# Scoring two heads at once, the queries' second parts in 64-row matmuls side by side

## The chip, the cores and the metric

The kernel runs on one core of a Trainium2 chip. The metric is the device time of one execution in microseconds (us); the time before is the median of three runs, 733.85 us (732.66 to 736.66). One further execution was recorded by the hardware profiler. TensorE is called PE, VectorE DVE, ScalarE ACT, GpSimd POOL and SyncE SP; PEld is TensorE's loading of weights, the stationary operand of a matmul.

## What is computed

Local attention with a few global keys and a bias that falls with the distance, over 4 sequences of 768 positions and 8 heads of 64 elements, and then a gated two-layer network on the result (3072 tokens, 512 wide, 1536 hidden):

```python
scores = scale * np.matmul(q, k.transpose(0, 1, 3, 2))
keep = is_global | is_local            # key j: j < 8, or 0 <= i - j < 96
scores = np.where(keep, scores - slopes[h] * dist, -1e9)
a = softmax(scores)
x = np.matmul(a, v)                    # heads side by side: 3072 x 512
out = ((x @ w_a) * (x @ w_b)) @ w_out
```

Everything is float32. A product of two float32 matrices is made from parts that TensorE multiplies in one pass: each operand is cut into a first part (rounded to the type float32r) and a second part (what is left), and the products of first with first, first with second and second with first are added up.

## The kernel before

**Units.** The 24 blocks of 128 queries are dealt into eight units: unit 0 has the first block of each sequence (4 blocks), unit 1 has 2 blocks, units 2 to 7 have 3 each. A query block needs a window of keys only: 232 keys (its own 128, the 96 before and the 8 global ones), or 128 for the first block of a sequence. For each unit the kernel computes attention, and then the network on the unit's tokens (`moe`, 12 steps of 128 hidden columns). While unit u is in the network, the attention of unit u + 1 is computed in between.

**The network** (L1042 and L1060) is TensorE's main load: per step two projections of 12 matmuls each, whose moving operand is as wide as the unit has tokens (512, 256 or 384), and per block three matmuls of 512 columns back into the accumulators acc.

**Attention of units 2 to 7** (`attention`, called late units below). Heads are taken one by one. For each head, SP loads a tile raw, whose rows 0 to 63 hold the head's queries (transposed) and one half of its keys, and whose rows 64 to 127 hold the same queries again and the other half of the keys. `split` (L582) makes three tiles of it: qh, the queries' first part, scaled, on all 128 rows; ql, their second part, also on all 128 rows; kk, in which each key column has its first part on one half of the rows and its second part on the other half. With this layout one matmul of 128 rows gives the queries' first part times both parts of the keys. For every window (a block and a head) there are two matmuls into the bank psS (L953): qh with kk, then ql with kk. DVE adds the bias to the scores and takes the row's extreme (L659, which reads the bank), ACT takes the exponential (L676), the row is divided by its sum (L708 or L710), DVE transposes blocks of 32x32 (L752), and 16 small transfers per pair of heads put those blocks in place in a tile pf (L766). Then the product with the values v (L787, `values`): a stationary operand of 64 columns, the even head of a pair in the columns 0 to 63 and the odd one in 64 to 127. Values of two pairs of heads are done in one go (JOINT = 2), into the banks psA and psT. L787 is float32 without parts; the trace lists two instructions for each float32 matmul.

**Attention of units 0 and 1** (`quad`) uses raw float32 tiles with two heads on the two halves of the rows: scores by matmuls of 64 rows (L821), the two heads into two banks, transposes on TensorE (L735), values by L787. This part is not touched by the change.

**The order of the work** is written by a planner inside the kernel. Every operation has a due time, a cost for each engine that may do it, and the buffers that it reads and writes; `Schedule.order` walks through modelled time and gives each engine its next operation whose inputs and buffers are there. The costs are constants in the code: `pe(n)` is n / 2.23 + 2.5 ns, and a score operation of a late unit has `2 * pe(w)`. A list of numbers, MOVES, shifts the due times of some operations of the first two units at random by fixed seeds. The result is a fixed order for each engine; on the chip an engine works through its list and waits where an input isn't there.

**Buffers that the change touches.** kk, qh and raw have two buffers, ql one, pf two. TensorE's eight result banks are psS, psT, psA, acc0 to acc2, p0 and p1, one buffer each.

## Time and profile before

| | |
|---|---|
| median of three runs | 733.85 us (732.66 to 736.66) |
| the profiled execution: its own time | 731.68 us |
| its span, first to last instruction | 729.8 us |
| granted TensorE clock | 0.999 |
| busy: PE / PEld / DVE / ACT / POOL | 97% / 88% / 66% / 48% / 1% |
| PE's work ends at | 723.5 us of the span |
| matmul instructions on PE | 4356 |

A row of the timeline gives the start and the duration of a group of instructions that follow each other. A matmul's duration includes its way through the array, during which the next ones already run, so what a matmul costs is read from the distance between two starts, not from its duration. "64*128" in a row is the shape of the stationary operand, rows by columns.

### The profile page before, as it was taken

What the parts mean: (1) busy time and instruction counts of PE and PEld (TensorE: products, weight loads), DVE (VectorE), ACT (ScalarE), POOL (GpSimd) and SP (SyncE); (2) the same over time, 40 slices, a digit from 0 to 9 for tenths busy, and PEclk for the clock granted to TensorE, in tenths of its full rate; (3) what the DMA queues carried; (4) which work ended last, traced back from release to release, by engine and by line L of the source; (5) the groups of instructions that cost most, each with busy time, mean ns of one, the idle gap of its engine ahead of it and who ended that gap; (6) DMA issues with size and microseconds to landing.
All of it is one profiled execution on the core that took longest, in us unless ns stands there. A gap on an engine that the chain in (4) does not pass through costs nothing.

```text
span 729.8 us, 12598 instructions
## 1 busy us (share of the span) xinstructions
PE 708.6 (97%) x4356; PEld 639.2 (88%) x4356; DVE 483.1 (66%) x1560; ACT 353.1 (48%) x907; POOL 5.9 (1%) x16
## 2 busy tenths in 40 slices
PE   5899999999999999999999999999999999999996
PEld 4577777899899999999899999998999999999996
DVE  6999999779975873587726967278662896321111
ACT  5999776364553552555426544263443554221111
POOL 3000000000000000000000000000000000000000
PEclk9999999999999999999999999999999999999999
DMA  7899100134543343134331343224432243110001
GB/s 269 316 380 364 41 17 28 42 101 127 170 137 81 90 129 108 64 89 125 89 104 65 106 129 108 65 85 106 135 101 86 65 128 88 45 44 1 1 1 48
DMA packets 38552, 78.06 MB, mean 107 GB/s; under 512 B 8528, under 2 KB 21072, under 8 KB 38480
## 3 DMA queue, kind: packets, MB, share of 16 engines
q1 hardware_dynamic: 28960, 67.33, 28.8%
q10 hardware_dynamic: 9520, 9.84, 5.3%
q8 instruction: 36, 0.59, 0.3%
q14 instruction: 36, 0.29, 0.1%
HBM read 51.97 MB, written 6.29 MB: 80 GB/s over the span
## 4 chain that ended last, share of the span: by engine, by line
PE 84%; DVE 5%; ACT 3%; DMA 3%; ACTq 2%; issue 1%; SPq 1%; DVEq 0%; POOL 0%; POOLq 0%
PE p L1042 49%; PE acc L1060 24%; PE pa L787 5%; PE ps L953 4%; DMA pf<-wm 3%; ACTq L766 2%; DVE t L659 1%; ACT t L676 1%; DVE wm L752 1%; ACT wr L516 1%; PE pt L735 1%; PE ps L821 1%; SPq L766 1%; DVE kk L447 1%; PE acc_2b L1060 1%
## 5 line engine op out<-in xcount | busy, mean ns | idle before, releaser
L1042 PE MATMUL p<-xh,wt 128*128 128x384 f32 (+2 forms) x1488 | 419.5, 337 | 1.4 <-ACT raw L437 0.9
L1042 PEld LDWEIGHTS p<-xh,wt 128*128 128x128 f32 x1488 | 271.0, 188 | 15.2 <-ACT raw L437 1.9
L1042 PE MATMUL p<-xl,wt 128*128 128x384 f32 (+2 forms) x816 | 269.7, 340 | 0.7 <-ACT xl L437 0.5
L1060 PE MATMUL acc<-wt,hh 128*128 128x512 f32 (+1 forms) x576 | 203.4, 390 | 0.0
L1042 PEld LDWEIGHTS p<-xl,wt 128*128 128x128 f32 x816 | 153.4, 188 | 10.8 <-ACT xl L437 0.8
L1060 PEld LDWEIGHTS acc<-wt,hh 128*128 128x128 f32 x576 | 108.3, 188 | 20.0 <-issue 1.6
L1081 DVE TENSOR_TENSOR raw<-p,raw 128x384 f32<-128x384 f32 (+2 forms) x96 | 52.9, 551 | 90.5 <-PE p L1042 89.7
L676 ACT ACTIVATE t<-t,sm 128x232 f32<-128x232 f32 (+1 forms) x120 | 55.3, 464 | 116.7 <-DMA pf<-wm 71.3
L1060 PE MATMUL acc<-wt,hl 128*128 128x512 f32 (+1 forms) x288 | 111.7, 388 | 0.0
L437 ACT COPY raw<-p 128x384 f32<-128x384 f32 (+2 forms) x71 | 34.4, 485 | 122.3 <-PE p L1042 116.2
L447 DVE TENSOR_TENSOR hl<-raw,hh 128x384 fp32r<-128x384 f32 (+2 forms) x96 | 52.8, 550 | 11.1 <-ACT hh L437 10.4
L1060 PEld LDWEIGHTS acc<-wt,hl 128*128 128x128 f32 x288 | 54.2, 188 | 6.6
L659 DVE CUSTOM_DVE_ANT_0 t<-ps,rel 128x232 f32<-128x232 f32 x74 | 28.8, 389 | 39.2 <-PE ps L953 38.4
L447 DVE TENSOR_TENSOR kk<-raw,kk 64x348 fp32r<-64x348 f32 x96 | 49.6, 516 | 3.6 <-ACT kk L437 0.5
L437 ACT CAST hh<-raw 128x384 fp32r<-128x384 f32 (+2 forms) x72 | 37.3, 519 | 19.8 <-DVE raw L1081 19.6
L787 PE MATMUL pa<-pf,v 128*64 128x128 f32 x640 | 41.5, 278 | 1.7 <-ACT pf L437 1.4
L787 PEld LDWEIGHTS pa<-pf,v 128*64 128x64 f32 x640 | 35.9, 138 | 7.2 <-issue 3.5
L953 PE MATMUL ps<-kk,qh 128*128 128x232 f32 x144 | 39.8, 277 | 1.5 <-DVE sm L659 1.5
L708 ACT ACTIVATE wm<-wm,sm 128x232 f32<-128x232 f32 x58 | 27.9, 487 | 24.6 <-DVE sm L698 23.9
L953 PE MATMUL ps<-kk,ql 128*128 128x232 f32 x144 | 39.5, 274 | 0.0
L676 ACT ACTIVATE wm<-wm,sm 128x232 f32<-128x232 f32 x72 | 34.7, 483 | 5.7 <-DVE sm L659 5.1
L708 ACT ACTIVATE t<-t,sm 128x232 f32<-128x232 f32 (+1 forms) x76 | 34.6, 477 | 5.1 <-DVE sm L698 4.0
(84 smaller groups left out, 687.4 us busy)
## 6 DMA issues: line engine op xcount, KB each, us to landing
wr<-wts SPq DMA_DIRECT2D x24, 768.0 KB, 10.9
raw<-qkv SPq DMA_DIRECT2D x48, 366.0 KB, 3.0
v<-qkv SPq DMA_DIRECT2D x24, 384.0 KB, 3.2
pf<-wm ACTq DMA_DIRECT2D x192, 48.0 KB, 2.0
pf<-wm SPq DMA_DIRECT2D x192, 48.0 KB, 1.9
out<-o SPq DMA_DIRECT2D x23, 256.0 KB, 2.0
v<-qkv SPq DMA_DIRECT2D x8, 256.0 KB, 3.9
raw<-qkv SPq DMA_DIRECT2D x3, 512.0 KB, 8.0
```

Of the source, the lines that this page charges most:

```text
L437: self.nc.scalar.copy(out(), src())
L447: lambda e: self.engine(e).tensor_sub(out(), a(), b()),
L516: lambda e, low=low: nc.scalar.activation(low(), low().bitcast(U32), AF.Copy, scale=2.0**-29),
L659: lambda e, j=j, o=o, w=w, neg=neg, at=at: nc.vector.tensor_tensor_reduce(t[:, o : o + w], ps[:, o : o + w], neg[:, at : at + w], -scale, ...
L676: lambda e, j=j, o=o, w=w: nc.scalar.activation(t[:, o : o + w], t[:, o : o + w], AF.Exp, bias=sm[:, j : j + 1], scale=-1.0, accum_out=sm[ ...
L708: nc.scalar.mul(t[:, o : o + w], t[:, o : o + w], r)
L766: lambda e, out=out, src=src: self.queue(e).dma_start(out(), src()),
L787: nc.tensor.matmul(pa[D * s : D * s + D, i * P : i * P + P], v[:, v0 : v0 + D], probs[s, i][1](c), start=c == 0, stop=c == len(slots) - 1,)
L953: nc.tensor.matmul(ps[:, :w], q[:, i * P : i * P + P], kk[:, k0 : k0 + w], start=m == 0, stop=m == 1,)
L1042: nc.tensor.matmul(p[:, :T], wt(), b[:, b0 : b0 + T], start=c == 0 and n == 0, stop=c == NCC - 1 and n == 2,)
L1060: nc.tensor.matmul(acc[:, :n], hs[:, i * P : i * P + P], wt(), start=f == 0 and k == 0, stop=f == NF - 1 and k == 2,)
L1081: lambda e, asb=asb, pb=pb: nc.vector.tensor_mul(asb[:, :T], pb[:, :T], asb[:, :T]),
```

## The change

**Scores.** The heads of a late unit are taken by pairs. The two raw tiles of a pair are packed differently: one has the first half of both heads' keys, the other the second half, the even head on rows 0 to 63 and the odd head on rows 64 to 127 (the queries of a tile are still those of one head, twice). `split` makes qh and kk for both heads, and one ql for the pair: the even head's second part on the rows 0 to 63, the odd head's on 64 to 127. In a head's kk, the keys' first part now stands on the rows of the head's own half for all columns. A score operation serves one block and both heads: qh with kk for the even head into psS, the same for the odd head into psT, then ql with kk on 64 rows for each of the two heads, into the same two banks. The product of the queries' second part with the keys' second part is left out. The planner's cost is `3 * pe(w) + 10`.

**Values** are done for one pair of heads at a time, always into psA. The results of the pairs 2 and 3 go into the pair's own pf tile instead of new tiles.

MOVES is another list. Softmax, transposes, transfers, the network and the units 0 and 1 have the same operations as before; the numbers of matmuls are the same.

```diff
@@ -40,10 +40,7 @@
 CHUNKS = 12
 SQ = 32
 
-JOINT = 2
-
-SHORT = PAIRED
-OLD = ()
+PBUFS = 2
 
 
 HOMES = "kk sm raw hh v wm hl xh xl o qh pf ql t"
@@ -76,7 +73,7 @@
...
-MOVES = (1010, 1025, 1037, 1048, 1089, 1106, 1156, 1251, 1276, 1371, 1475, 1603, 1662, 1754, 1881, 11792, 12402, 7, 26, 46, 60, 85, 142, 169, 213, 252, 392, 531, 549, 595, 835, 995, 2161, 2240, 11001)
+MOVES = (8, 33, 56, 90, 167, 201, 230, 264, 328, 358, 418, 533, 564, 621, 754, 4891, 5013, 5338, 5407)
...
@@ -579,51 +576,57 @@
         )
         return v
 
-    def split(self, u, h, due, raw):
+    def split(self, u, c, due, raws):
+
 
 
         nc, pl, op = self.nc, PLANS[u], self.plan.op
         nq, hk = pl.nb * P, pl.nk // 2
-        n = f"{u}_{h}"
-        reads = [raw]
-        sc = 2.0 ** (h - 2)
-        qh = self.sbuf([P, MAXQ], F32R, "qh", "qh" + n, 2)
-        ql = self.sbuf([P, MAXQ], F32R, "ql", "ql" + n)
-        kk = self.sbuf([P, MAXK], F32R, "kk", "kk" + n, 2)
-
-        def scale(e):
-            if e == "act":
-                nc.scalar.mul(qh[:, :nq], raw[:, :nq], sc)
-            else:
-                nc.vector.tensor_scalar_mul(qh[:, :nq], raw[:, :nq], sc)
-
-        op(due, scale, reads, [qh], port=BOTH, act=act(nq), dve=dve(nq, True))
-        op(
-            due,
-            lambda e: nc.vector.scalar_tensor_tensor(
-                ql[:, :nq], raw[:, :nq], sc, qh[:, :nq], op0=ALU.mult, op1=ALU.subtract
-            ),
-            reads + [qh],
-            [ql],
-            port=BOTH,
-            dve=dve(nq),
-        )
-        for half in range(2):
-            a, o = slice(64 * half, 64 * half + 64), slice(64 - 64 * half, 128 - 64 * half)
+        halves = slice(0, 64), slice(64, 128)
+        ql = self.sbuf([P, MAXQ], F32R, "ql", f"ql{u}_{c}")
+        qhs, kks = [], []
+        for s, raw in enumerate(raws):
+            h = 2 * c + s
+            sc = 2.0 ** (h - 2)
+            qh = self.sbuf([P, MAXQ], F32R, "qh", f"qh{u}_{h}", 2)
+            qhs.append(qh)
+            kks.append(self.sbuf([P, MAXK], F32R, "kk", f"kk{u}_{h}", 2))
+
+            def scale(e, raw=raw, qh=qh, sc=sc):
+                if e == "act":
+                    nc.scalar.mul(qh[:, :nq], raw[:, :nq], sc)
+                else:
+                    nc.vector.tensor_scalar_mul(qh[:, :nq], raw[:, :nq], sc)
+
+            op(due, scale, [(raw, "q")], [qh], port=BOTH, act=act(nq), dve=dve(nq, True))
+            op(
+                due,
+                lambda e, raw=raw, qh=qh, sc=sc, a=halves[s]: nc.vector.scalar_tensor_tensor(
+                    ql[a, :nq], raw[a, :nq], sc, qh[a, :nq], op0=ALU.mult, op1=ALU.subtract
+                ),
+                [(raw, "q"), qh],
+                [(ql, s)],
+                port=BOTH,
+                dve=dve(nq),
+            )
+
+        for half, raw in enumerate(raws):
             cols = slice(half * hk, half * hk + hk)
-            src = lambda a=a: raw[a, pl.k0 : pl.k0 + hk]
-            hi = lambda a=a, cols=cols: kk[a, cols]
-            self.copy(due, hi, src, hk, reads, [(kk, (half, 0))])
-            self.sub(
-                due,
-                lambda o=o, cols=cols: kk[o, cols],
-                src,
-                hi,
-                hk,
-                reads + [(kk, (half, 0))],
-                [(kk, (half, 1))],
-            )
-        return qh, ql, kk
+            for s, kk in enumerate(kks):
+                a, o = halves[s], halves[1 - s]
+                src = lambda raw=raw, a=a: raw[a, pl.k0 : pl.k0 + hk]
+                hi = lambda kk=kk, a=a, cols=cols: kk[a, cols]
+                self.copy(due, hi, src, hk, [(raw, "k")], [(kk, (half, 0))])
+                self.sub(
+                    due,
+                    lambda kk=kk, o=o, cols=cols: kk[o, cols],
+                    src,
+                    hi,
+                    hk,
+                    [(raw, "k"), (kk, (half, 0))],
+                    [(kk, (half, 1))],
+                )
+        return qhs, ql, kks
 
     def dist(self, h):
 
@@ -906,7 +909,7 @@
             self.result(1, c, due + step, pa, x)
 
     def probs32(self, name):
-        return self.sbuf([P, CHUNKS * P], F32, "pf", name, JOINT)
+        return self.sbuf([P, CHUNKS * P], F32, "pf", name, PBUFS)
 
     def result(self, u, c, due, pa, x):
         nq, (xc, x0) = PLANS[u].nb * P, x[c]
@@ -929,72 +932,65 @@
             x += [(self.probs32(f"x{u}_{c}"), 0) for c in range(2, NCC)]
             self.second(x, start, end)
             return x
-        step = (end - start) / H
+        step = (end - start) / NCC
+        each = sum(len(slots) for slots in pl.vslot)
         groups = []
         for c in range(NCC):
+            due = start + c * step
             probs = {}
-            v = self.fetch_v(u, c, start + (2 * c + 1) * step - LOADLEAD)
+            v = self.fetch_v(u, c, due + step / 2 - LOADLEAD)
             pf = self.probs32(f"pf{u}_{c}")
+            raws = [self.fetch(u, 2 * c + s, due - LOADLEAD) for s in range(2)]
+            qhs, ql, kks = self.split(u, c, due - SPLITLEAD, raws)
             slot = 0
-            old = u == SHORT and c in OLD
-            for s in range(2):
-                h = 2 * c + s
-                due = start + h * step
-                raw = self.fetch(u, h, due - LOADLEAD)
-                qh, ql, kk = self.split(u, h, due - SPLITLEAD, raw)
-                for i in range(pl.nb):
-                    due = start + h * step + (i + 1) * step / pl.nb
-                    k0, w = pl.kwin[i]
-                    n = f"{u}_{h}_{i}"
-                    ps = self.bank("psS", "ps" + n)
-
-                    def scores(e, i=i, k0=k0, w=w, ps=ps, qh=qh, ql=ql, kk=kk):
-                        for m, q in enumerate((qh, ql)):
-                            nc.tensor.matmul(
-                                ps[:, :w],
-                                q[:, i * P : i * P + P],
-                                kk[:, k0 : k0 + w],
-                                start=m == 0,
-                                stop=m == 1,
-                            )
-
-                    op(due, scores, [qh, ql, kk], [ps], pe=2 * pe(w), spare=SPARE)
-                    turn = (pl.nb * h + i) % (TBUFS + len(self.spares))
+            for i in range(pl.nb):
+                due = start + c * step + (i + 1) * step / pl.nb
+                k0, w = pl.kwin[i]
+                n = f"{u}_{c}_{i}"
+                ps = [self.bank(tag, f"{tag}{n}") for tag in ("psS", "psT")]
+
+                def scores(e, i=i, k0=k0, w=w, ps=ps, qhs=qhs, ql=ql, kks=kks):
+                    qs = slice(i * P, i * P + P)
+                    for s in range(2):
+                        nc.tensor.matmul(
+                            ps[s][:, :w], qhs[s][:, qs], kks[s][:, k0 : k0 + w], start=True, stop=False
+                        )
+
+                    for s in range(2):
+                        r = slice(64 * s, 64 * s + 64)
+                        nc.tensor.matmul(
+                            ps[s][:, :w], ql[r, qs], kks[s][r, k0 : k0 + w], start=False, stop=True
+                        )
+
+                op(due, scores, [*qhs, ql, *kks], ps, pe=3 * pe(w) + 10, spare=SPARE)
+                chunks = len(pl.vslot[i])
+                for s in range(2):
+                    h = 2 * c + s
+                    turn = (2 * (pl.nb * c + i) + s) % (TBUFS + len(self.spares))
                     if turn < TBUFS:
-                        t = self.sbuf([P, 2 * P], F32, "t", "t" + n, TBUFS)
+                        t = self.sbuf([P, 2 * P], F32, "t", f"t{s}{n}", TBUFS)
                     else:
                         t = self.spares[turn - TBUFS]
-                    sm = self.sbuf([P, 8], F32, "sm", "sm" + n, 6)
+                    sm = self.sbuf([P, 8], F32, "sm", f"sm{s}{n}", 6)
                     dist = lambda w: (self.negd if w > P else self.negd0, 0)
                     done = [(self.wm, k) for k in range(MBUFS)]
-                    self.softmax(due, [(0, w)], ps, t, sm, dist, 2.0 ** -(h + 1), done, REST)
-                    chunks = len(pl.vslot[i])
-                    if old:
-                        pt = self.bank("psT", "pt" + n)
-                        self.turn(due, [(0, w)], t, pt, pf, slot * P, SPARE)
-                    else:
-                        self.blocks32(due, w, t, slot, chunks)
-
-                    def get(k, slot=slot, pf=pf, old=old):
-                        if old:
-                            return pf[:, (slot + k) * P : (slot + k + 1) * P]
+                    self.softmax(due, [(0, w)], ps[s], t, sm, dist, 2.0 ** -(h + 1), done, REST)
+                    at = s * each + slot
+                    self.blocks32(due, w, t, at, chunks)
+
+                    def get(k, at=at, pf=pf):
                         view = pf[:, :].rearrange("p (a m i) -> p m a i", a=P // SQ, m=CHUNKS)
-                        return view[:, slot + k]
+                        return view[:, at + k]
 
                     probs[s, i] = (pf, get)
-                    slot += chunks
-            due = start + (2 * c + 2) * step
-            if not old:
-                self.swap(due, pf, slot)
-            pa = self.bank(("psA", "psT")[c % JOINT], f"pa{u}_{c}")
-            groups.append((v, probs, pa))
-            if len(groups) == JOINT:
-                self.values(due, pl, range(pl.nb), groups)
-                if len(x) <= c:
-                    x += [(self.probs32(f"x{u}_{k}"), 0) for k in range(2, NCC)]
-                for k, (_, _, pa) in enumerate(groups, c + 1 - JOINT):
-                    self.result(u, k, due, pa, x)
-                groups = []
+                slot += chunks
+            due = start + (c + 1) * step
+            self.swap(due, pf, 2 * each)
+            pa = self.bank("psA", f"pa{u}_{c}")
+            self.values(due, pl, range(pl.nb), [(v, probs, pa)])
+            if len(x) <= c:
+                x.append((pf, 0))
+            self.result(u, c, due, pa, x)
         return x
 
     def moe(self, u, start, step, x):
@@ -1443,8 +1439,9 @@
         if u >= PAIRED:
             hk = pl.nk // 2
             for h in range(H):
-                rows = (kt[h][:, :hk], kt[h][:, hk:])
-                put(QOFFS[u][h], np.vstack([np.hstack([qt[h], half]) for half in rows]))
+                half = slice(h % 2 * hk, h % 2 * hk + hk)
+                pair = kt[h - h % 2], kt[h - h % 2 + 1]
+                put(QOFFS[u][h], np.vstack([np.hstack([qt[h], k[:, half]]) for k in pair]))
         else:
             for c in range(NCC):
                 cols = []
```

**How the order on PE changes.** The first place is in unit 3's attention, in between the network of unit 2 (xh and p are the network's, acc its accumulators). Before, the two matmuls of one window, for head 2 and block 1, with the network's ahead and behind:

```order
L1060 MATMUL acc2_2_2786<-wt1_1_764,hl2_1_2796 128x512
L1060 MATMUL acc2_2_2786<-wt1_1_764,hh2_1_2790 128x512
L953 MATMUL ps3_2_1_2871<-kk3_2_2635,qh3_2_2627 128x232
L953 MATMUL ps3_2_1_2871<-kk3_2_2635,ql3_2_2808 128x232
L1042 MATMUL p02_3_2874<-xh2_2606,wt3_0_941 128x384
L1042 MATMUL p02_3_2874<-xl2_2613,wt3_0_941 128x384
```

Now the operation for block 1 and the heads 2 and 3:

```order
L1038 MATMUL p12_3_2864<-xh2_2598,wt3_1_978 128x384
L955 MATMUL psS3_1_1_2906<-kk3_2_2793,qh3_2_2785 128x232
L955 MATMUL psT3_1_1_2908<-kk3_3_2795,qh3_3_2787 128x232
L961 MATMUL psS3_1_1_2906<-kk3_2_2793,ql3_1_2798 128x232
L961 MATMUL psT3_1_1_2908<-kk3_3_2795,ql3_1_2798 128x232
L1056 MATMUL acc2_0_2750<-wt2_1_848,hh2_2_2844 128x512
```

Two of the four score matmuls (L961) now have a stationary operand of 64 rows; ahead of them and behind them stand matmuls of 128 rows. There are 144 score operations before and 72 now, all of this form.

The second place is the end of unit 2's attention, where the values of its pairs 2 and 3 are. Before:

```order
L1042 MATMUL p02_0_2622<-xh2_2606,wt0_0_636 128x384
L787 MATMUL pa2_2_2651<-pf2_2_2325,v2_2_2312 64x128 x12
L787 MATMUL pa2_3_2664<-pf2_3_2536,v2_3_2341 64x128 x12
L1060 MATMUL acc1_0_1791<-wt11_1_1572,hh1_11_2620 128x512
L1060 MATMUL acc1_0_1791<-wt11_1_1572,hl1_11_2637 128x512
```

Now, pair 2 some 65 rows earlier, and pair 3:

```order
L1038 MATMUL p01_10_2466<-xl1_1701,wt10_0_1531 128x256
L1038 MATMUL p01_10_2466<-xh1_1682,wt10_0_1531 128x256
L790 MATMUL pa2_2_2488<-pf2_2_2363,v2_2_2044 64x128 x12
L1038 MATMUL p01_10_2466<-xh1_1682,wt10_0_1531 128x256
...
L1056 MATMUL acc1_1_1844<-wt11_1_1627,hh1_11_2609 128x512
L790 MATMUL pa2_3_2650<-pf2_3_2545,v2_3_2274 64x128 x12
L1038 MATMUL p02_0_2621<-xh2_2598,wt0_0_636 128x384
```

What was one block of 24 matmuls of 64 columns is now two blocks of 12, each between the network's matmuls; over the late units there are 24 such blocks instead of 12.

## The prediction

> **What bounds the kernel now.** I read the page's totals first, then busy time by stage, then the waits of TensorE (PE), then single starts on PE. From the page:
>
> ```profile
> span 729.8 us, 12598 instructions
> PE 708.6 (97%) x4356; PEld 639.2 (88%) x4356; DVE 483.1 (66%) x1560; ACT 353.1 (48%) x907; POOL 5.9 (1%) x16
> PE 84%; DVE 5%; ACT 3%; DMA 3%; ACTq 2%; issue 1%; SPq 1%; DVEq 0%; POOL 0%; POOLq 0%
> ```
>
> The busy times of stretches of the span (the stretch, its length, then the engines); the late units' attention lies in the second of them:
>
> ```profile
> 42.00:145.00 103.00, 103.00 (x512) 81.49 (x511) 98.46 (x191) 74.84 (x136) 0.00 (x0) 1.00 0.37 139
> 145.00:640.00 495.00, 492.85 (x3181) 458.56 (x3180) 331.68 (x1174) 226.67 (x628) 0.00 (x0) 1.00 0.36 100
> 640.00:723.50 83.50, 83.44 (x472) 79.10 (x470) 16.58 (x31) 17.20 (x35) 0.00 (x0) 1.00 0.03 10
> ```
>
> From 145 to 640 us PE stands still for 2.2 us of 495, and DVE, the next one, is busy for 67%. So whatever the change adds to PE or takes from it there comes out at the end one for one, unless another engine becomes late. PE's longest waits, by sum (us, times, longest); of the late units' score operations (L953) it is the third:
>
> ```profile
> PE ps L821 <- DMA raw<-qkv: 5.1, 1, 5.1
> PE ps L821 <- DVE sm L659: 2.0, 1, 2.0
> PE ps L953 <- DVE sm L659: 1.5, 3, 0.7
> ```
>
> "Busy" hides one thing: how far apart the starts are. That is where this change acts.
>
> **What a score operation costs now.** Single starts on PE (start, duration, instruction), in unit 4's attention:
>
> ```profile
> 303.82 0.34 PE L1042 MATMUL p<-xl,wt 128*128 128x384 f32 x1
> 303.99 0.34 PE L1042 MATMUL p<-xh,wt 128*128 128x384 f32 x1
> 304.16 0.27 PE L953 MATMUL ps<-kk,qh 128*128 128x232 f32 x1
> 304.27 0.28 PE L953 MATMUL ps<-kk,ql 128*128 128x232 f32 x1
> 304.38 0.34 PE L1042 MATMUL p<-xh,wt 128*128 128x384 f32 x1
> 304.56 0.34 PE L1042 MATMUL p<-xl,wt 128*128 128x384 f32 x1
> ```
>
> The starts follow each other without a break: 0.17 us for a projection, 0.11 for each score matmul. From 303.99 to 304.56 are 0.57 us; less the two projections (0.17 and 0.18) a window costs 0.22, so two windows cost 0.45 (0.44 and rounding).
>
> **What a change of the stationary operand's shape costs.** The new matmuls have 64 rows and stand between matmuls of 128 rows, 72 times. The trace has such places: units 0 and 1 score with 64 rows (L821), two heads side by side. One of unit 1's:
>
> ```profile
> 112.43 0.40 PE L1060 MATMUL acc<-wt,hl 128*128 128x512 f32 x1
> 112.66 0.39 PE L1060 MATMUL acc<-wt,hh 128*128 128x512 f32 x1
> 112.98 1.05 PE L821 MATMUL ps<-raw 64*128 64x232 f32 x8
> 113.97 0.51 PE L1060 MATMUL acc<-wt,hh 128*128 128x512 f32 x1
> 114.31 0.40 PE L1060 MATMUL acc<-wt,hl 128*128 128x512 f32 x1
> ```
>
> Narrow looks at the same block show when a row's first instruction is the second of the second pair, and then of the third pair:
>
> ```profile
> 113.29 0.55 PE L821 MATMUL ps<-raw 64*128 64x232 f32 x3
> 113.49 0.55 PE L821 MATMUL ps<-raw 64*128 64x232 f32 x3
> ```
>
> So a pair follows a pair after 0.20 us, and the four pairs should take 0.78 (0.196 each). From 112.66 to 114.31 are 1.65; less two matmuls of acc (0.23 each, 112.43 to 112.66) that is 1.19. **About 0.40 us of it is no matmul at all.** It comes in three pieces: the first 64-row matmul starts 0.32 after the last one of 128 rows instead of 0.23; the first pair takes 0.31 instead of 0.20; and behind the block the next start comes some 0.09 late, and the one after it at 0.34 instead of 0.23. I read this as: the array runs empty, then the first weights of the new shape are loaded with nothing to cover them (weights are otherwise loaded under the matmul before), and the same again on the way back.
>
> The values (L787, 64 columns) allow a check with two sizes, 16 and 48 instructions:
>
> ```profile
> 57.39 0.40 PE L1060 MATMUL acc<-wt,hh 128*128 128x512 f32 x1
> 57.72 1.09 PE L787 MATMUL pa<-t,v 128*64 128x128 f32 x16
> 58.74 0.51 PE L1060 MATMUL acc<-wt,hh 128*128 128x512 f32 x1
> 59.09 0.40 PE L1060 MATMUL acc<-wt,hl 128*128 128x512 f32 x1
> ...
> 373.36 0.40 PE L1060 MATMUL acc<-wt,hh 128*128 128x512 f32 x1
> 373.68 2.84 PE L787 MATMUL pa<-pf,v 128*64 128x128 f32 x48
> 376.45 0.51 PE L1060 MATMUL acc<-wt,hh 128*128 128x512 f32 x1
> 376.80 0.40 PE L1060 MATMUL acc<-wt,hl 128*128 128x512 f32 x1
> ```
>
> Less the two neighbours the blocks cost 1.70 - 0.46 = 1.24 and 3.44 - 0.46 = 2.98. The difference, 1.74 for 32 instructions, is 0.054 each; 16 of them make 0.87. So 0.37 us of a block is independent of its size, here too. Is it the shape, or that these are plain float32 among float32r? The transposes are float32 with a full 128*128:
>
> ```profile
> 51.80 0.86 PE L1042 MATMUL p<-xl,wt 128*128 128x512 f32 x3
> 52.50 0.60 PE L735 MATMUL pt<-ident,t 128*128 128x128 f32 x4
> 52.88 0.50 PE L1042 MATMUL p<-xh,wt 128*128 128x512 f32 x1
> 53.22 0.40 PE L1042 MATMUL p<-xl,wt 128*128 128x512 f32 x1
> ```
>
> The three before them start at 51.80, so the transposes come in on time (3 x 0.23 = 0.70), and from 52.50 to 53.22 less one projection are 0.49 for four of some 0.11 each: 0.05 lost, not 0.4. It is the shape.
>
> **The change part by part.**
>
> *Scores.* Per pair of windows: two full matmuls (0.22), one side-by-side pair of 64 rows, and the fixed 0.40. What a float32r pair of 64 rows takes no row shows. Above: it runs one after the other, 0.22. Below: as quick as one full matmul, 0.10 to 0.11. The rows are near the lower: a transpose takes 0.11 for 128 columns, 0.85 ns a column, while L821 takes 0.196 for two instructions of 232 columns, 0.42 ns each, and so they do overlap. I take 0.10. That makes 0.72 against 0.45, or +0.27 us, and 72 times that is **+19.4 us**. The saved quarter of the matmuls is in it: 72 x 0.11 = 7.9 us less, against 72 x 0.40 = 28.8 us more (the sums differ by rounding). Bounds of the fixed part: no row has a change of shape between float32r and float32r, so from nothing to 0.41.
>
> *Values.* The late units have 24 blocks of 24 instructions instead of 12 of 48. The instructions stay as many; the fixed part comes 12 times more: 12 x 0.37 = **+4.4 us**. At a unit's end the last pair's values now have 12 projections (2.1 us) ahead of the first matmul that reads them, before it was 3.4 us of work; copy, cast and subtraction take about 0.5 us each, so at one place up to 0.5 us may be waited. I count none.
>
> *DVE and ACT.* The numbers of operations stay: per head one qh, one ql (64 rows instead of 128, the same 384 columns), four each of the casts and subtractions of kk over a pair. Hidden as now under PE's 495 us; without that cover DVE has 163 us to spare there.
>
> *Waits.* A score operation now waits until DVE has read both banks of the one before, 0.39 us and 0.08 for each window by these rows, so 0.95 together:
>
> ```profile
> L659 DVE CUSTOM_DVE_ANT_0 wm<-ps,rel 128x232 f32<-128x232 f32 x72 | 28.1, 391 | 12.2 <-PE ps L953 12.0
> L659 DVE DVE_READ_ACCUMULATOR2_ANT sm<- 128x1 f32 x192 | 15.9, 83 | 0.0
> ```
>
> Behind a waiting score operation stand the network's matmuls, so such a wait would count in full. But the new order has 12 or more network matmuls between two score operations, 9 at one place: nine projections of 0.17 and three matmuls of acc at 0.23 make 2.2 us, somewhat less in unit 1 with its narrower projections. With half as many operations that need the banks I rather expect the 1.5 us of waits shown above to shrink than to grow. I count nothing either way, 1.5 us of gain and 1.5 of loss as the bounds. Loads: the raw tiles are loaded two at a time now, the same bytes; a pair has some 20 us for it (495 us for 24 pairs), and the one wait of PE for a load (5.1 us, for L821) is at the start, in unit 0.
>
> *First units and end.* Operations as before, in a slightly other order (other MOVES). PE idles 12.7 us in the first 42 us and 6.3 us at the end (729.8 - 723.5). I take both as unchanged, with 2 us of doubt.
>
> ```profile
> 0.00:42.00 42.00, 29.30 (x195) 20.07 (x196) 35.97 (x166) 34.24 (x109) 5.93 (x16) 1.00 0.81 292
> ```
>
> **Sum.** The profiled execution took 731.68 us, span 729.8 and 1.9 around it. 731.7 + 19.4 + 4.4 = 755.5. The median of the runs lies 2.2 above that execution, which would make 757.6. I predict **756 us**, 3% slower; the cases' own range is 752 to 760.
>
> **What the notes say.** The Trainium skill, TensorEngine Tiling (Array Packing), has both sides: its Overview (Theoretical Speedup) gives up to twice the speed where the contracted dimension is at most 64, by which alone the scores would gain the 7.9 us and the time be 728; its Key Properties say that changing the tiling mode, not just the tile, drains TensorE. The trace agrees with the second: every change of shape shows the empty array (0.32 for 0.23), and the weights' reload on top, which that page doesn't price.
>
> **Rivals.**
>
> *No price between float32r and float32r* (7%). One mechanism: the array is emptied only because L821 and L787 are issued in two passes, and single-pass matmuls of 64 rows slip in behind full ones. Against it: the float32 transposes come in free, and L787 and L821, with different shapes, pay the same 0.37 to 0.40. For it: no row with this type. Then 731.7 - 7.9 + 4.4 = 728, or 730 from the median: faster. The point from which it decides: per score operation 0.45 - 0.32 = 0.13 is saved without the price, 0.06 goes to the values (4.4 / 72), so the change is not slower only if less than 0.07 of the 0.40 is left.
>
> *Half the price* (8%): the array is emptied each way (0.09 to 0.10), but the weights of both 64-row matmuls are loaded under the full ones, and the next projection's under them, as elsewhere; of 0.40 are left 0.19. Then 72 x (0.32 + 0.19 - 0.45) = 4.3, with the values 8.7: 740 to 743.
>
> *No overlap* (6%): the two 64-row matmuls run one after the other, so that the change doesn't do what it says. 72 x 0.1 = 7.2 more: 763 to 765. Against it the 0.42 ns per column above.
>
> *Attention falls late* (3%): both heads of a pair need both raw tiles and all four kk parts before the first score, since kk and qh have two buffers and a pair takes both. If PE waited 1 us for that at each of the 24 pairs, it would be 780. Against it: DVE has room, and PE, slower than the planner thinks, gives it more.
>
> **How the numbers follow.** The forecast has 76%. A range of 8 in 10 takes 752 to 760 and reaches out to the doubt on the pair and the first units on either side: 747 to 764. What is below (728, 741) and above (780) is 18%. A measurement of this kernel can tell about 0.5% (3.7 us) from no change. Faster by more: the first rival, 6%. Within: its rest, 2%. Slower: 92%.
>
> **What would show it.** In the changed kernel's timeline the first 64-row score matmul should start about 0.20 after the full one ahead of it (not 0.11), its two instructions some 0.01 apart, the next projection about 0.29 after them, and the one after that 0.28 later (not 0.17): 0.72 for a score operation beside its neighbours. PE's busy time should grow by about 23 us, since these losses lie inside the modelled durations, and its idle time stay near 21 us; DVE's and ACT's busy times stay. I am wrong on the main step if the projection behind a score operation follows at 0.11, on the pair if the two instructions start 0.1 apart, and on the cover if PE's waits for DVE grow by more than 3 us.

## The result: 2.9% slower

| | before | changed |
|---|---|---|
| median | 732.97 us (731.35 to 736.66, 6 runs) | 754.52 us (753.79 to 755.17, 6 runs) |
| ratio, 95% interval | | 1.029 (1.0264 to 1.0315) |
| profiled execution, its span | 731.68, 729.8 us | 753.79, 752.0 us |

The forecast was 756. From the page of the changed kernel:

```profile
span 752.0 us, 12628 instructions
PE 730.9 (97%) x4356; PEld 641.0 (85%) x4356; DVE 482.6 (64%) x1549; ACT 357.9 (48%) x908; POOL 15.3 (2%) x26
```

PE is busy for 22.3 us more (730.9 - 708.6) with as many instructions, and idle for 21.1 us as before (21.2). DVE's busy time is the same within 0.5 us; ACT's is 4.8 us longer and POOL's 9.4, since the planner gave POOL nine subtractions (L444). The whole loss is in the time that PE calls busy. In the stretch of the late units' attention PE stands still for 1.7 us of 520:

```profile
145.00:665.00 520.00, 518.33 (x3200) 463.81 (x3199) 331.09 (x1159) 228.01 (x623) 7.96 (x8) 1.00 0.33 95
```

One of the new score operations on PE's timeline (start, duration, instruction), between the network's matmuls:

```profile
343.08 0.39 PE L1056 MATMUL acc<-wt,hh 128*128 128x512 f32 x1
343.31 0.27 PE L955 MATMUL psS<-kk,qh 128*128 128x232 f32 x1
343.42 0.28 PE L955 MATMUL psT<-kk,qh 128*128 128x232 f32 x1
343.62 0.37 PE L961 MATMUL psS<-kk,ql 64*128 64x232 f32 x1
343.63 0.37 PE L961 MATMUL psT<-kk,ql 64*128 64x232 f32 x1
343.93 0.45 PE L1038 MATMUL p<-xh,wt 128*128 128x384 f32 x1
344.21 0.34 PE L1038 MATMUL p<-xl,wt 128*128 128x384 f32 x1
344.39 0.51 PE L1038 MATMUL p<-xh,wt 128*128 128x384 f32 x2
```

The full matmuls follow each other after 0.11. The first one of 64 rows comes 0.20 after the full one, its partner at once. Then the next projection starts 0.30 later, and the second projection 0.28 after that, where 0.17 is usual. From 343.08 to 344.21 are 1.13 us; less 0.23 and 0.17 that is 0.73 for the operation.

The weight loads (PEld) of the same operation show what the price is made of:

```profile
343.08 0.19 PEld L955 LDWEIGHTS psS<-kk,qh 128*128 128x128 f32 x1
343.32 0.19 PEld L955 LDWEIGHTS psT<-kk,qh 128*128 128x128 f32 x1
343.62 0.18 PEld L961 LDWEIGHTS psS<-kk,ql 64*128 64x128 f32 x1
343.93 0.19 PEld L1038 LDWEIGHTS p<-xh,wt 128*128 128x128 f32 x1
```

The weights of a full matmul behind a full one are loaded ahead of it, under the matmul before: from 343.08 for the start at 343.31, from 343.32 for the one at 343.42. Those of the 64 rows begin at 343.62, together with their own matmul, and those of the next projection at 343.93 likewise. So at each change of shape nothing covers the first load, as the prediction read it from unit 1's L821.

Over all operations after 145 us, with the two neighbouring matmuls' own time taken off in the same way, the medians are 0.227 us for one window before (144 operations) and 0.724 for a pair of windows now (71; one more lies before 145 us).

A block of values now, one pair of heads:

```profile
427.91 0.34 PE L1038 MATMUL p<-xh,wt 128*128 128x384 f32 x1
428.18 1.53 PE L790 MATMUL pa<-pf,v 128*64 128x128 f32 x24
429.64 0.44 PE L1038 MATMUL p<-xh,wt 128*128 128x384 f32 x1
429.92 0.34 PE L1038 MATMUL p<-xl,wt 128*128 128x384 f32 x1
```

From 427.91 to 429.92 less two projections: 1.66 us, the median of all 24 blocks. The old blocks of twice the size have 2.97 as their median.

**Where the 22.3 us of span went**, from the distances between the starts in the two profiled executions:

| part of PE's time | before | changed | difference |
|---|---|---|---|
| score operations at their median | 144 x 0.227 = 32.6 | 72 x 0.724 = 52.1 | +19.5 |
| what score operations took above it | 4.5 | 0.1 | -4.4 |
| values of the late units at their median | 12 x 2.973 = 35.7 | 24 x 1.663 = 39.9 | +4.2 |
| what values took above it | 0.0 | 0.7 | +0.7 |
| up to the network's first matmul | 30.6 | 31.5 | +1.0 |
| the rest: the network's delays, small parts, the end | | | +1.3 |

### The profile page after: what moved, and what is told of

Read it like the earlier page. It is cut to its first block, busy times and chain, and to the rows that moved or that the text cites. A ratio compares the mean times of both kernels' runs of the same rounds, so it can differ in the third digit from the quotient of the medians.

```text
span 752.0 us, 12628 instructions
## 1 busy us (share of the span) xinstructions
PE 730.9 (97%) x4356; PEld 641.0 (85%) x4356; DVE 482.6 (64%) x1549; ACT 357.9 (48%) x908; POOL 15.3 (2%) x26
## 4 chain that ended last, share of the span: by engine, by line
PE 85%; DVE 7%; ACT 3%; DMA 2%; ACTq 1%; issue 1%; DVEq 0%; POOL 0%; POOLq 0%; SPq 0%
PE p L1038 50%; PE acc L1056 24%; PE pa L790 5%; PE psS L961 3%; DVE kk L444 1%; ACTq L769 1%; DMA pf<-wm 1%; PE psT L955 1%; PE psS L955 1%; PE pt L738 1%; PE ps L824 1%; DVE wm L755 1%; DVE t L662 1%; ACT wr L513 1%; DMA raw<-qkv 1%
## 5 line engine op out<-in xcount | busy, mean ns | idle before, releaser
L1038 PE MATMUL p<-xh,wt 128*128 128x384 f32 (+2 forms) x1488 | 411.3, 341 | 1.2 <-ACT raw L434 0.7
L1056 PEld LDWEIGHTS acc<-wt,hh 128*128 128x128 f32 x576 | 108.2, 188 | 22.2 <-issue 1.3
L679 ACT ACTIVATE t<-t,sm 128x232 f32<-128x232 f32 (+1 forms) x120 | 55.3, 464 | 129.0 <-DMA pf<-wm 85.6
L444 DVE TENSOR_TENSOR hl<-raw,hh 128x384 fp32r<-128x384 f32 (+2 forms) x95 | 52.5, 553 | 11.4 <-ACT hh L434 10.5
L444 DVE TENSOR_TENSOR kk<-raw,kk 64x348 fp32r<-64x348 f32 x88 | 45.4, 516 | 2.5
L790 PE MATMUL pa<-pf,v 128*64 128x128 f32 x640 | 44.1, 280 | 2.4 <-ACT pf L434 1.5
L434 ACT CAST hh<-raw 128x384 fp32r<-128x384 f32 (+2 forms) x63 | 32.7, 519 | 23.4 <-DVE raw L1077 23.3
L679 ACT ACTIVATE wm<-wm,sm 128x232 f32<-128x232 f32 x72 | 34.6, 481 | 18.4 <-DVE sm L662 18.2
L662 DVE CUSTOM_DVE_ANT_0 t<-psS,rel 128x232 f32<-128x232 f32 x48 | 18.8, 393 | 37.6 <-PE psT L961 36.8
L434 ACT CAST kk<-raw 64x348 fp32r<-64x348 f32 x87 | 40.9, 478 | 1.2
L436 DVE COPY raw<-p 128x384 f32<-128x384 f32 (+1 forms) x24 | 12.6, 523 | 37.2 <-PE p L1038 37.0
L711 ACT ACTIVATE t<-t,sm 128x232 f32<-128x232 f32 (+1 forms) x68 | 31.2, 475 | 8.1 <-DVE sm L694 5.8
L755 DVE STREAM_TRANSPOSE wm<-wm 128x256 f32<-128x256 f32 x72 | 30.5, 433 | 5.5 <-ACT wm L711 4.7
```

Source lines behind the costliest of these rows:

```text
L434: self.nc.scalar.copy(out(), src())
L444: lambda e: self.engine(e).tensor_sub(out(), a(), b()),
L662: lambda e, j=j, o=o, w=w, neg=neg, at=at: nc.vector.tensor_tensor_reduce(t[:, o : o + w], ps[:, o : o + w], neg[:, at : at + w], -scale, ...
L679: lambda e, j=j, o=o, w=w: nc.scalar.activation(t[:, o : o + w], t[:, o : o + w], AF.Exp, bias=sm[:, j : j + 1], scale=-1.0, accum_out=sm[ ...
L711: nc.scalar.mul(t[:, o : o + w], t[:, o : o + w], r)
L755: nc.vector.transpose(dst, src)
```

## Experiments

In every run the kernel before ran on the same chip, and differences are to its median there (732.08 to 732.88 us). "Operation" is a score operation, and its time is the median of its trace, worked out as above.

### The shape of the second part undone

```diff
-                        r = slice(64 * s, 64 * s + 64)
                         nc.tensor.matmul(
-                            ps[s][:, :w], ql[r, qs], kks[s][r, k0 : k0 + w], start=False, stop=True
+                            ps[s][:, :w], ql[:, qs], kks[s][:, k0 : k0 + w], start=False, stop=True
                         )
```

> The changed kernel with one thing undone: the second score matmul of each head takes all 128 rows of ql and kk, not 64. The order of the work stays. The sum gets one small product more (the other head's second part of the queries with this head's second part of the keys), which is not in the reference. Theory (the price is in the change of the stationary operand's shape): a score operation of 0.725 us becomes four full matmuls, 4 x 0.107 = 0.43, so 72 x 0.295 = 21 us less: 733. Rival (the 22 us come from the order: pairs in two banks, loads by two, values by single pairs, another list of moves): it stays at 754. In between would share it out.

Measured: 739.57 us, 7.0 above the kernel before (732.62; ratio 1.0092, 1.0073 to 1.0112), 15 below the changed kernel. An operation on PE's timeline:

```profile
486.27 0.33 PE L1037 MATMUL p<-xh,wt 128*128 128x384 f32 x1
486.44 0.27 PE L955 MATMUL psS<-kk,qh 128*128 128x232 f32 x1
486.54 0.28 PE L955 MATMUL psT<-kk,qh 128*128 128x232 f32 x1
486.66 0.28 PE L960 MATMUL psS<-kk,ql 128*128 128x232 f32 x1
486.77 0.27 PE L960 MATMUL psT<-kk,ql 128*128 128x232 f32 x1
486.88 0.34 PE L1037 MATMUL p<-xh,wt 128*128 128x384 f32 x1
487.06 0.34 PE L1037 MATMUL p<-xl,wt 128*128 128x384 f32 x1
```

Four full matmuls cost less than two full ones and two side by side: the median operation is 0.451 instead of 0.724, 72 x 0.273 = 19.7 us. So the operation's price belongs to the shape. But the time fell by 15 only, not by 21. In the profiled execution (741.12 us, the longest of the four) values took 4.5 us above their median, and the network's delays were 2.1 us longer than in the changed kernel; I read this as PE coming to other work before its inputs are there. This part of the expectation was wrong; it comes back below.

### Two changes of shape per operation

```diff
                     for s in range(2):
                         nc.tensor.matmul(
                             ps[s][:, :w], qhs[s][:, qs], kks[s][:, k0 : k0 + w], start=True, stop=False
                         )
-
-                    for s in range(2):
                         r = slice(64 * s, 64 * s + 64)
```

> The changed kernel with the four matmuls of a score operation in the order even 128 rows, even 64, odd 128, odd 64, so that the shape changes there and back twice per operation instead of once. Theory (0.40 us per excursion to the other shape, whatever is in it): two excursions of 0.40 and two 64-row matmuls one after the other, 2 x (0.107 + 0.40 + 0.10) = 1.21 instead of 0.725, 72 x 0.49 = 35 us more: 789. Rival (a price per score operation, for instance of the first weights after a wait): only the lost overlap, 72 x 0.1 = 7 us more: 762.

Measured: 786.44 us, one execution.

```profile
514.39 0.33 PE L1036 MATMUL p<-xh,wt 128*128 128x384 f32 x1
514.56 0.26 PE L955 MATMUL psS<-kk,qh 128*128 128x232 f32 x1
514.75 0.37 PE L959 MATMUL psS<-kk,ql 64*128 64x232 f32 x1
515.05 0.37 PE L955 MATMUL psT<-kk,qh 128*128 128x232 f32 x1
515.36 0.37 PE L959 MATMUL psT<-kk,ql 64*128 64x232 f32 x1
515.65 0.44 PE L1036 MATMUL p<-xh,wt 128*128 128x384 f32 x1
515.93 0.34 PE L1036 MATMUL p<-xl,wt 128*128 128x384 f32 x1
```

From one change to the next the starts are 0.30 apart: 0.10 of work and 0.20 of price. The median operation is 1.210, as expected (1.21), 35 us in all; the time rose by 32; most of the difference is in the network's late delays, which fell from 4.3 us in the changed kernel's trace to 1.8. The price goes with each change of shape, not with the operation.

### Both 64-row matmuls on the same rows

```diff
-                        r = slice(64 * s, 64 * s + 64)
+                        r = slice(0, 64)
```

> The changed kernel with both 64-row matmuls of a score operation on the rows 0 to 63 (of ql and of each head's kk), so that they cannot run side by side; the odd head's second part is left out, and the even head's stands in its place. Shapes, order and number of matmuls stay. Theory (the two run side by side, 0.003 us apart): the second one follows the first after its own 0.10 us, 72 x 0.10 = 7 us more than the changed kernel: 761.5. Rival (the hardware gave no overlap worth having, and the short distance is only how starts are recorded): 754.5 as before. Second rival (the second one's weights cannot be loaded under the first on the same rows): 0.2 per operation, 769.

Measured: 762.09 us, one execution; the median operation is 0.831. This kernel leaves out the odd head's second part.

```profile
503.62 0.28 PE L955 MATMUL psT<-kk,qh 128*128 128x232 f32 x1
503.83 0.37 PE L961 MATMUL psS<-kk,ql 64*128 64x232 f32 x1
504.04 0.27 PE L961 MATMUL psT<-kk,ql 64*128 64x232 f32 x1
504.24 0.44 PE L1038 MATMUL p<-xh,wt 128*128 128x384 f32 x1
504.52 0.34 PE L1038 MATMUL p<-xl,wt 128*128 128x384 f32 x1
```

Together the distances grow by 0.11 against the changed kernel. So the two did run side by side, and that is worth 0.11 us per operation, 7.7 us in all. The second follows the first after 0.21, twice its own 0.10; the other half is the wait of the first for its weights, whose load starts at 503.83 with it, while that of the second's starts at 503.94, 0.10 ahead of its matmul. In the next distance of 0.20 I read the other half as the way back.

### Two blocks share one change of shape

```diff
+                        runs = [(two[0], True), (two[0], False)]
+                        if len(two) == 2:
+                            runs += [(two[1], False), (two[1], True)]
+                        for k, (m, hi) in enumerate(runs):
...
+                                r = slice(0, P) if hi else slice(64 * s, 64 * s + 64)
+                                nc.tensor.matmul(
+                                    ps[s][:, o : o + w],
+                                    (qhs[s] if hi else ql)[r, qs],
+                                    kks[s][r, k0 : k0 + w],
+                                    start=k % 2 == 0,
+                                    stop=k % 2 == 1,
+                                )
```

> The changed kernel with the blocks 0 and 1 of a pair in one score operation (block 2 alone as before), in the order: block 0 with 128 rows, block 0 with 64, block 1 with 64, block 1 with 128, so that two blocks share one excursion to the other shape. As many matmuls. Theory (0.40 us for an excursion, however many matmuls it holds): 24 excursions fewer, 24 x 0.40 = 9.6 us less, 745; an operation over two blocks takes 4 x 0.107 + 2 x 0.10 + 0.40 = 1.03 us. Up to 3 us of waits may come back, since PE becomes quicker. Rival (the price goes with each pair of 64-row matmuls): 754, as the changed kernel.

Measured: 746.26 us, 14.2 above the kernel before (ratio 1.0189, 1.0169 to 1.0209), where the changed kernel is 21.6 above it. The operation over two blocks:

```profile
488.33 0.28 PE L963 MATMUL psT<-kk,qh 128*128 128x232 f32 x1
488.54 0.37 PE L963 MATMUL psS<-kk,ql 64*128 64x232 f32 x1
488.54 0.37 PE L963 MATMUL psT<-kk,ql 64*128 64x232 f32 x1
488.75 0.27 PE L963 MATMUL psS<-kk,ql 64*128 64x232 f32 x1
488.76 0.27 PE L963 MATMUL psT<-kk,ql 64*128 64x232 f32 x1
488.95 0.38 PE L963 MATMUL psS<-kk,qh 128*128 128x232 f32 x1
489.17 0.28 PE L963 MATMUL psT<-kk,qh 128*128 128x232 f32 x1
489.28 0.34 PE L1044 MATMUL p<-xh,wt 128*128 128x384 f32 x1
```

Its median is 1.058 us where two single ones take 1.448, and the single ones left still take 0.722. 24 times 0.39 are 9.4 us less, of which 7.4 show in the time; in the profiled execution values and network took 2.2 us more than in the changed kernel's. A second pair of 64 rows adds almost nothing to the price: 1.058 less four full matmuls (0.107 each) and two pairs (0.10 each) leaves 0.43, where one pair left 0.40. What it would take for the 64 rows to pay is an estimate from these numbers: a side-by-side pair saves 0.11 against full matmuls and an excursion costs 0.40 to 0.43, so it takes four such pairs per excursion to come out even. No score operation tried here has that many. A bank of 512 columns holds two windows of 232.

### Values by single pairs alone

In the kernel before:

```diff
-            pa = self.bank(("psA", "psT")[c % JOINT], f"pa{u}_{c}")
-            groups.append((v, probs, pa))
-            if len(groups) == JOINT:
-                self.values(due, pl, range(pl.nb), groups)
...
+            pa = self.bank("psA", f"pa{u}_{c}")
+            self.values(due, pl, range(pl.nb), [(v, probs, pa)])
+            if len(x) <= c:
+                x.append((pf, 0))
+            self.result(u, c, due, pa, x)
```

> The kernel before with one part of the change alone: values by single pairs of heads, into psA, results of the pairs 2 and 3 into the pair's own pf. Theory (0.36 us for each of 12 more blocks of 64 columns): 4.3 us more than before, 737.3 against 733.0. Rival (as many matmuls, so as much time; the order absorbs it): 733.

Measured: 745.71 us, 13.1 more than before (732.62; ratio 1.0181, 1.0163 to 1.0198). Three times the expectation. Among PE's waits are now some for the values, which the kernel before doesn't have in its late units:

```profile
PE pa L787 <- ACT t L676: 2.2, 1, 2.2
PE ps L953 <- DVE sm L659: 1.9, 4, 0.6
PE pa L787 <- issue: 1.5, 2, 1.3
```

The list of moves belongs to another program: its seeds draw operations by their place in the list of operations, and draw others here. And the trace has something else besides waits: for 10.2 us from 220.9 us on, around the wait of 2.2 us, PE had half its clock and was busy for 8.9 us of them (see the last section). So the same with a list chosen for it:

```diff
-MOVES = (1010, 1025, 1037, 1048, 1089, ...)
+MOVES = (1025, 1037, 1048, 1106, 1251, 1371, 1475, 1603, 1881, 7, 26, 85, 169, 252, 531, 595, 916, 10664, 4125)
```

> Values by single pairs in the kernel before, as in the run that did this part alone, but with another list of moves, chosen for this program by the planner's own count. Theory (12 more changes of shape cost 4.3 us; the other 8 us of that run were waits of an order whose list of moves was chosen for another program): 737 to 738. Rival (the smaller blocks bring the waits by themselves, because a block now stands close behind its transfers): 745 again.

Measured: 739.07 us, 6.2 more than before (732.88; 1.0076, 1.0055 to 1.0096), a little above the expected range and far from the rival's 745. A block of 24 instructions has a median of 1.665 us in this trace, so 24 x 1.665 - 12 x 2.973 = 4.3, the expected price. What is above 4.3 I take for waits: in this trace blocks of values took 4.9 us above their median, and score operations less than in the kernel before. Of the first run's 8.8 us over the price its order made most, by waits and by the half clock around them; 1.9 stayed.

### Pairs with full rows: can they beat the kernel before?

Both heads into one bank, values for two pairs:

```diff
-                ps = [self.bank(tag, f"{tag}{n}") for tag in ("psS", "psT")]
+                ps = self.bank("psS", f"ps{n}")
...
+                        for m, q in enumerate((qhs[s], ql)):
+                            nc.tensor.matmul(
+                                ps[:, s * 256 : s * 256 + w],
+                                q[:, qs],
+                                kks[s][:, k0 : k0 + w],
+                                start=m == 0,
+                                stop=m == 1,
+                            )
...
-                op(due, scores, [*qhs, ql, *kks], ps, pe=3 * pe(w) + 10, spare=SPARE)
+                op(due, scores, [*qhs, ql, *kks], [ps], pe=4 * pe(w), spare=SPARE)
...
+            pa = self.bank(("psA", "psT")[c % 2], f"pa{u}_{c}")
+            groups.append((v, probs, pa, pf))
+            if len(groups) == 2:
+                self.values(due, pl, range(pl.nb), [g[:3] for g in groups])
```

> Pairs of heads as in the changed kernel, but the second parts with all 128 rows (with the small product more, as in the run with full rows), both heads of an operation in one bank, psS, side by side in its columns, and values for two pairs at once as before. No change of shape is left in the scores, and half of the changes for the values. Theory: the changed kernel less 21 (scores) less 4.4 (values), 729, thus 4 us below the kernel before, since score operations by pairs also wait less for a free bank (before, 19 of 144 score operations took 4.6 us more than the others by their starts). Rival (one bank for two heads brings the waits back): 733 or more.

Then with a list of moves chosen for it, then in addition with SPARE, the planner's slack ahead of score and value operations, at 500 and at 900 ns instead of 200 (each with its own list):

> Score operations by pairs with 128 rows in one bank, values for two pairs at once, with a list of moves chosen for this program. Theory (the 9 us over the sum in the first run of this design were waits of its order): 729 to 732, below or at the kernel before. Rival (the one bank brings the waits of the score operations, 4 us, and they stay whatever the order): 735 to 738.

> Score operations by pairs with 128 rows in one bank and values for two pairs at once, as in the two runs of this design, with 0.5 us instead of 0.2 us of slack in the planner's count ahead of score and value operations, and a list of moves for it. Theory (what is left over the kernel before are waits in places where the planner's count is too tight): 730 to 733. Rival (the waits belong to the design: when TensorE has less to do, the pair's own chain through DVE, ACT and the transfers is late next, whatever slack is planned): 735 to 738.

> The design of pairs with 128 rows in one bank and joint values, with 0.9 us of slack and a list of moves chosen for it. With 0.5 us it took the time of the kernel before; its trace still had 2.3 us of waits of score operations and 2 us of the network's projections. Theory (more slack takes the rest of the score operations' waits): 730 to 732. Rival (the rest isn't where the slack is planned): 732 to 734.

And the changed kernel with full rows, two banks and single values, priced as four matmuls and with its own list:

> The changed kernel with 128 rows for the second parts, two banks and values by single pairs, the planner's cost for a score operation set to four full matmuls, and a list of moves chosen for this program. Theory: the kernel before, plus 4.3 for the values, less up to 4 for the waits for a bank: 733 to 735, thus 20 to 21 below the changed kernel, the whole price of the shape less the saved matmul. Rival (the waits of the first run with full rows belong to the faster scores, not to the order): 739 to 740 again.

| run | median | to the kernel before | ratio, 95% interval |
|---|---|---|---|
| one bank, joint values, list of the changed kernel | 738.16 | +5.5 | 1.0077 (1.0059 to 1.0095) |
| the same, its own list | 736.35 | +3.5 | 1.0042 (1.0026 to 1.0058) |
| the same, slack 500 | 732.74 | +0.7 | 1.001 (0.9997 to 1.0022) |
| the same, slack 900 | 735.53 | +2.8 | 1.0044 (1.0027 to 1.0061) |
| two banks, single values, its own list | 738.13 | +5.3 | 1.0062 (1.0044 to 1.0081) |

In all four one-bank runs the operation's median is 0.45 and that of a joint block of values 2.97 to 2.98, so PE's own work is that of the kernel before. I expected 729 to 732 in the first two since pairs would wait less for a bank; that was wrong. In the trace of the second, an execution of 739.8 us, score operations still took about 3.7 us above their median (before: 4.5), and the network's late delays were 8.6 us instead of 3.1. With a slack of 500 the first fell to 2.3 and the second to 5.1, and the time, 732.74, is at the end of the expected 730 to 733. With 900 the first was 2.2 us, but the network's delays were longer again, among them waits of 1.4 us and 1.1 us in unit 1's network, and the time is above what either guess had.

What is left lies ahead of unit 2's network. Its first projection starts at 208.1 us before, and at 214.9, 209.7 and 214.7 us in the runs with the own list, slack 500 and slack 900; from there to the last projection it takes 510.9 us before and 511.8, 510.9 and 510.3 in these. Some of it is ahead of everything that the change touches: the network's first matmul comes at 33.1, 31.8 and 33.1 us instead of 30.6. So what remains lies in the stretch of the first two units, and what sets it there isn't settled. The design comes to the kernel before and not below it.

The last run of the table, with two banks and single values, missed its 733 to 735: with a list of its own it is only 1.4 us quicker than the first run with full rows (739.57), so this list didn't take those waits away. In its trace values took 2.2 us and score operations 1.3 us above their medians.

Is the slack worth anything without the pairs?

```diff
-SPARE = 200.0
+SPARE = 500.0
-MOVES = (1010, 1025, 1037, 1048, 1089, ...)
+MOVES = (1156, 1251, 1276, 1371, 1603, 1662, 1754, 1881, 7, 85, 142, 213, 392, 595, 2161, 11001, 9114, 13280, 10065, 16357, 7103, 15884)
```

> The kernel before with nothing changed but the planner's slack ahead of the late units' score and value operations, 0.5 us instead of 0.2, and a list of moves chosen for it. It asks whether slack by itself brings a gain, or only undoes the waits of operations by pairs. Theory (the 4.5 us that 19 of the 144 score operations wait for the one bank are a matter of the planner's slack): 728 to 731. Rival (one bank for windows one by one leaves DVE no time, whatever slack is planned): 732 to 735.

Measured: 729.82 us against 732.76 (ratio 0.9954, 0.9938 to 0.997). This is the quickest of all kernels here, 0.5% below the kernel before and 3.3% below the changed one. The theory of the waits isn't shown by it, though: in its trace score operations still took 3.9 us above their median, against 4.5. Whether the gain comes from the slack or from the new list wasn't tried apart.

## Why the prediction was right, point by point

- **PE bounds, and what it loses comes out one for one.** Right: +22.3 us busy, +22.2 us of span, idle time as before, and PE's listed waits for DVE sum to 5.7 us, before to 5.4. In the other direction it didn't hold here: taking work from PE (the run with full rows) gave back 15 of 20 us.
- **0.45 us for two windows, 0.72 for the new operation.** Right: 0.45 and 0.724. The term came to 19.5 us, forecast 19.4. Its parts as forecast from unit 1's L821: the 64-row matmul 0.20 after the full one, its partner at once, the next projection 0.30 later (forecast 0.29), the one after that at 0.28.
- **The overlap**, taken at 0.10 from the columns per ns of other rows: right, the run on the same rows cost 7.7 us more, where the rival was priced at 7.2.
- **The price between float32r and float32r**, of which the trace had no row: the full 0.40. The transposes, float32 with a full shape, had pointed there. The rivals without the price (728) and with half of it (741, the weights loaded under other matmuls) fall by the rows above. The Trainium skill's sentence in TensorEngine Tiling (Array Packing), Key Properties, that changing the tiling mode drains TensorE, agrees with the 0.20 before the first 64-row matmul instead of 0.11; the page's factor of up to two for 64 rows (Overview, Theoretical Speedup) holds between the two matmuls (0.11 us) and is lost to the change.
- **Values**: forecast +4.4, measured +4.2 at the median and 0.7 of waits.
- **The mis-sized term: waits of the score operations.** I counted nothing, with 1.5 us of gain as the bound, from the list of waits. By the starts, 19 of the 144 operations before took 4.6 us longer than the rest, and that went to 0.1. The list counts from the modelled end of the matmul ahead to the next start, which leaves out a part. One case of before:

```profile
357.27 0.34 PE L1042 MATMUL p<-xh,wt 128*128 128x384 f32 x1
358.32 0.38 PE L953 MATMUL ps<-kk,qh 128*128 128x232 f32 x1 [0.71 <-DVE sm L659]
358.53 0.27 PE L953 MATMUL ps<-kk,ql 128*128 128x232 f32 x1
```

  The list has 0.71. From 357.27 to 358.32 are 1.05 instead of 0.17, and the next matmul comes after 0.21 instead of 0.11: 0.98 lost. So the forecast was 4.4 too high there; the first units and the network's small delays, taken as unchanged, and the values' waits were 3.0 us too low (1.0, 1.3 and 0.7 in the table). They cancel in part, which is why 755.5 met a profiled 753.8 so closely: the term of the shape was right, the closeness of the sum is partly luck.
- **Attention falls late** (780): not in the changed kernel, whose PE is slower than the planner counts (0.72 us for an operation, planned at about 0.33). The quicker variants had waits too, but not of this kind: by their lists PE waited for what the values read, for a bank or for the network's inputs, not for the parts of a pair's keys.

## What to carry to other kernels

Cost a matmul by the distance between starts, and look for a place in the same trace where the stationary operand changes shape: here each way there and back cost 0.37 to 0.43 us, with 2 to 48 instructions in between, as much as four full matmuls of 232 columns. By the estimate above, half-height matmuls would pay only in longer runs of their own shape than were tried here. And when the bound engine got slower, the sum from rows held; when it got quicker, part of the gain came back as waits in other places, and how much of it depended on the order.

## What was not expected of the hardware

A wait of PE may cost more than itself. In the run with full rows PE waited for a transfer, and the granted clock (the third number from the end) was 0.50 for the 3.4 us that followed:

```profile
293.80:296.20 2.40, 0.15 (x3) 0.12 (x4) 0.56 (x1) 0.94 (x2) 0.00 (x0) 1.00 0.40 104
296.20:299.60 3.40, 3.40 (x26) 3.07 (x27) 0.56 (x1) 0.52 (x2) 0.00 (x0) 0.50 0.02 5
```

```profile
293.47 0.40 PE L1055 MATMUL acc<-wt,hh 128*128 128x512 f32 x1
296.11 2.78 PE L790 MATMUL pa<-pf,v 128*64 128x128 f32 x24 [2.25 <-DMA pf<-wm]
298.82 0.69 PE L1037 MATMUL p<-xh,wt 128*128 128x384 f32 x1
```

The block of values took 2.71 us from its start to the next one instead of 1.46 as above. With the wait that place lost 3.8 us. A wait of 0.6 us, in the changed kernel, left the clock at 1.0.

It isn't the only place. In the traces of before and changed kernel, from 16 us on, the clock of 0.50 comes only after PE's last matmul. But values by single pairs alone had it for 10.2 us from 220.9 us on, the one-bank run with its own list for 3.4 us from 204.6 us on, behind waits of 1.7 and 0.5 us, and six runs had it for 3.4 or 6.8 us, beginning at 29 to 34 us, in the first units. So part of what is called waits above is work at half speed. How long a wait must be isn't shown: at 31 us the changed kernel waited 0.93 us and went on at 1.0, the run with two blocks in one operation waited 0.96 us at the same place and had 0.50 from 31.4 us on.
